# Block-causal attention and gated MLP on one core: maxima over partitions taken by GpSimd instead of TensorE matmuls, scales of q, k and v formed from the maximum itself

## The chip, the cores and the metric

The kernel runs on one core of a Trainium2 chip. The metric is device time in microseconds (us) of one execution, the median of the runs. One core has five engines that matter here, each with its own instruction queue that runs strictly in order: TensorE (PE in the profile; its weight loads stand apart as PEld), VectorE (DVE), ScalarE (ACT), GpSimd (POOL) and SyncE (SP), which only issues DMA transfers. TensorE writes its results to PSUM; VectorE and ScalarE take them from there.

## The reference

```
scores = scale * q @ k.T                      # per batch (8) and head (8), 576 x 576, head size 64
scores = where(block_i >= block_j, scores, -1e9)   # blocks of 64
attn   = softmax(scores);  a = attn @ v
x      = a as (8*576 tokens, 512)
h      = x @ w_in                             # 512 -> 2048
out    = (h * clip(h + 3, 0, 6) / 6) @ w_out  # 2048 -> 512
```

q, k, v and the output are float32. The weights arrive as 64-bit floats, and the kernel itself converts them.

## The kernel before, in words

**Precision.** Most of the work runs as float16 products in three terms: an operand x is scaled, split into a high part hi = f16(x*s) and a low part lo = f16(x*s - hi), and a product becomes hi*hi + hi*lo + lo*hi. The scale s of each operand is made on the chip, from the data: for each pair of heads for q and k, for each batch for v, for each of 8 chunks of the two weight matrices. The first batch (and the first piece of the MLP) runs in float32 without scales, while the weights are still being converted.

**Stages.** There are 8 batches of 4 head pairs: 32 slots, n = 0 to 31. Slots 0 to 3 take the float32 path (`qk_load32`, `qk_prep32`, `s_block32`, `t_block32`, `pv_group32`). Slots 4 to 31 take the float16 path: `qk_load` loads q and k of a head pair; `qk_prep` makes the scales, splits q and k and sends them through a transposing DMA to the tile qkT; `s_group` forms the scores on TensorE (tile s), takes row maxima on VectorE (st), the exponentials on ScalarE (p), splits the probabilities (ph, phl) and transposes them by DMA (pT); `v_max` and `v_prep` scale and split v (vhl); `pv_group` multiplies (pv) into x. The tokens are cut into 13 pieces for the MLP: `ffn1` forms h (tile h; from piece 10 on by seven products in place of eight, tile u, from sums made by `w_forms` and `x_forms` on VectorE), `ffn2` the output (o, osb). The attention of later batches and the MLP of earlier ones run side by side, so that TensorE always has one of them.

**The order.** No engine chooses its order on the chip. The function emits its operations to a `Recorder`, each with a due time (`nc.key`, from the tables and constants at the top of the file: `AT` for the slots, `FT` for the pieces, `QP`, `VP`, `M0`, `S0` and so on as offsets), and with a cost that the planner holds for it. `Recorder.schedule` (lines 296 to 492) simulates the engines with these costs and writes one fixed order for each; an operation that can run on several engines goes to the one that the plan finds free first. All engine instructions but the first memsets are issued from line 498, so the profile names them L498 and is read by tile names.

**The scales.** `pow2_scale` (line 569) makes a scale from the per-partition figures mx of 128 partitions and one or two columns. Everything that follows needs the same value in each partition. In `qk_prep` mx is the sum of absolute values of each partition, made by ScalarE; for v and the weights it is the true maximum (v) or again a sum (weights):

- q and k (`exact=False`): one joint pair of small float32 matmuls with a matrix of ones adds mx over the partitions into PSUM (tile mb_q); then VectorE, in its queue: `am` (lower bound), `pw` (exponent bits alone, a power of two), `rs` twice (product with 2^-14, reciprocal), and `esc` (the factor of the exponent).
- v and weights (`exact=True`): a pair of matmuls with the identity first transposes mx (mt_v, mt_w), VectorE takes the maximum along the row (`dg`) and spreads it on a diagonal, a second pair with ones brings it to all partitions (mb_v, mb_w), and the same chain follows.

With the 16 scales of v and w and the 28 of q and k, 44 scales are made. The option `far`, by DMA through memory, is never taken (`WFAR, VFAR = 99, 99`). GpSimd has only memsets to do: the zero halves of the float32 q tiles (`qkf`, at the start), and zero blocks of the probabilities (`pf`, `p`).

`w_max` calls `pow2_scale` for a chunk of weights, `w_split` uses the result; their due times are M0 + i*MD and S0 + i*SD for i = 0 to 7. `qk_prep` of slot n is due QP slots ahead of its `s_group`, `v_prep` VP slots behind the slot's start.

Of the kernel before, what the change touches and what calls it, by code (L numbers as in the profile page):

```python
# [10 lines left out]
F32 = mybir.dt.float32  # L11
# [3 lines left out]
ALU = mybir.AluOpType  # L15
AX = mybir.AxisListType

P = 128
# [4 lines left out]
WX = 14  # L23
WY = 27

U = 0.632
AS = (6.363, 13.291, 20.163, 24.432)
AL = 17.497
PV0 = 2.428
TA, TR, PR = 2.701, 4.807, 2.397  # L30
QR = 4.605
PVA, PVB = 0.974, 1.579
PHS = 18
WLP = 0
WHA = 0
EXA = 8
QTH = False
EVR = 3
EVP = 0
PRO = True  # L40
MEM = 0
BIASV = 262.216
WFAR, VFAR = 99, 99
SW = 10
WF0, WFD = 768.607, 15.583
XFA = 10.306

NMIN = 64
QL = -4.051
VL = -0.654  # L50
W0, WD = 11.216, 2.584
S0, SD = 56.335, 3.846
M0, MD = 33.747, 5.394
RT = (28.905, 39.268, 48.982, 59.104)
RS, RL, VL1 = 1.915, 15.575, 37.318
VM0, VMX = 80.864, 0.114
AT = ((4, 86.25), (5, 104.31), (6, 123.19), (8, 163.76), (9, 178.32), (10, 199.81), (12, 251.29), (13, 269.94), (14, 285.88), (15, 306.89), (16, 332.9), (24, 564.98), (32, 785.9))
FT = ((0, 34), (1, 120.0), (2, 165.17), (3, 233.37), (4, 273.76), (5, 348.85), (6, 400.52), (7, 495), (10, 765), (13, 965.63))
UNI = False
QP = 0.642  # L60
VP = 0.443
BLK = 64
EXPONENT_BITS = 0x7F800000

# [19 lines left out]
        return call  # L84


ADV = {("tensor", "a"): 51.29}


class Recorder:  # L90
# [15 lines left out]
    def __init__(self, nc):  # L106
        self.nc = nc
        self.ops = []
        self.key = 0.0
        self.cls = ""  # L110
        self.joint = None
        self.adv = ADV
        self.BIAS = {"vector": BIASV, "gpsimd": 500.0}
        for n in self.NAMES:
            setattr(self, n, Engine(self, n))
        self.hist = {}
        self.meta = {}
        self.users = {}
# [121 lines left out]
    def cost(self, eng, method, args, kw, outs, ins):  # L240


        n = self.count(outs[0])
        if method == "dma_start":
            nb = mybir.dt.size(outs[0].dtype)
            for _, c in list(outs[0].ap):
                nb *= c
            if kw.get("transpose"):
                occ = max(1290, 189 * nb / 32768 - 200)
                return occ, occ + (1100 if nb <= 4 * 32768 else 2100), False  # L250
            if eng == "gpsimd":
                return 1300, 2900 + nb / 170, False
            return 600, 2000 + nb / 170, False
        if eng == "vector":
            if method == "tensor_reduce":
                n = self.count(ins[0])
            else:
                ptr = any(isinstance(a, bass.AP) and self.count(a) == 1 for a in args[2:] if n > 1)
                ptr = ptr or n == 1 and method == "tensor_scalar_mul" and isinstance(args[2], bass.AP)
            wide = [a for a in ins if self.count(a) > 1 and not self.psum(a)]  # L260
            port = len(wide) > 1
            if method in ("tensor_scalar", "tensor_copy") and n > 1:
                if not any(self.psum(a) for a in outs + ins):
                    if len(outs[0].ap) == 2 or outs[0].ap[1][1] % 2 == 0:
                        n = n / (4 if mybir.dt.size(outs[0].dtype) + mybir.dt.size(ins[0].dtype) == 4 else 2)
                        port = True
            occ = 68 + 1.042 * n
            if method != "tensor_reduce" and ptr:
                occ += 57
            return occ, occ + 80, port  # L270
        if eng == "scalar":
            occ = 94 + 0.8335 * n
            if isinstance(kw.get("scale"), bass.AP):
                occ += 95
            if isinstance(kw.get("bias"), bass.AP):
# [226 lines left out]
def kernel(  # L502
# [13 lines left out]
    nc = Recorder(tc.nc)  # L516
    B, H, S, D = q.shape
# [23 lines left out]
    E_P = 2.0 ** 14  # L541
    E_X = 2.0 ** -14
    E_G = 2.0 ** -25
    C_EXP = (D ** -0.5) * 2.0 ** -28
    C_H = 2.0 ** -28
    C_O = 2.0 ** -17 / 6.0
    TINY = 1e-18


# [2 lines left out]
    natp = ctx.enter_context(tc.tile_pool(name="nat", bufs=2))  # L552
    attp = ctx.enter_context(tc.tile_pool(name="att", bufs=2))
    ffp = ctx.enter_context(tc.tile_pool(name="ff", bufs=3))
    drp = ctx.enter_context(tc.tile_pool(name="dr", bufs=2, space=bass.MemoryType.DRAM))
    ps_s = ctx.enter_context(tc.tile_pool(name="ps_s", bufs=3, space=bass.MemoryType.PSUM))
    ps_h = ctx.enter_context(tc.tile_pool(name="ps_h", bufs=2, space=bass.MemoryType.PSUM))
    ps_o = ctx.enter_context(tc.tile_pool(name="ps_o", bufs=1, space=bass.MemoryType.PSUM))
# [7 lines left out]
    ph01 = [wpool.tile([P, 2, PT_U[g], P], F16, tag=f"ph{g}", name=f"ph{g}") for g in range(2)]  # L566
    padded = []

    def pow2_scale(mx, n, nm, to=None, exact=False, far=False):

# [7 lines left out]
        if exact and far:  # L578
            row = drp.tile([n, P], F32, tag=f"row{n}", name=f"dr_row_{nm}")
            nc.sync.dma_start(row.rearrange("n p -> p n"), mx)  # L580
            al = sm.tile([P, n, P], F32, tag="al", bufs=1, name=f"al_{nm}")
            nc.sync.dma_start(
                al.rearrange("p n x -> p (n x)"),
                row.rearrange("n p -> (n p)").rearrange("(o x) -> o x", o=1).to_broadcast([P, n * P]),
            )
            nc.vector.tensor_reduce(am, al, axis=AX.X, op=ALU.max)
            nc.vector.tensor_scalar_max(am, am, TINY)
        else:
            if exact:
                pt_ = ps_s.tile([P, 512], F32, tag="s", name=f"mt_{nm}")  # L590
                nc.joint = "mt", nm
                for h in range(2):
                    wide = mx[:, h % n:h % n + 1].to_broadcast([P, BLK])
                    nc.tensor.matmul(pt_[h * BLK:(h + 1) * BLK, :P], wide, ident, start=True, stop=True)
                nc.joint = None
                dg = sm.tile([P, n + 1], F32, tag=f"dg{n}", name=f"dg_{nm}")
                nc.vector.tensor_reduce(dg[:, n:], pt_[:, :P], axis=AX.X, op=ALU.max)
                nc.vector.tensor_scalar_mul(dg[:, :n], ident[:, :(n - 1) * BLK + 1:BLK], dg[:, n:])
                mx = dg[:, :n]
            ps = ps_s.tile([P, 512], F32, tag="s", name=f"mb_{nm}")  # L600
            nc.joint = "mb", nm
            for h in range(2):
                nc.tensor.matmul(ps[h * BLK:(h + 1) * BLK, :n], ones[:, :BLK], mx, start=True, stop=True)
            nc.joint = None
            nc.vector.tensor_scalar_max(am, ps[:, :n], TINY)
        nc.vector.tensor_scalar(
            pw.bitcast(I32), am.bitcast(I32), EXPONENT_BITS, None, op0=ALU.bitwise_and
        )
# [26 lines left out]
    ones = one.to_broadcast([P, P])  # L635
    three = wpool.tile([P, 1], F32, tag="three", name="three")
    nc.gpsimd.memset(three, 3.0)
    n_raw = []
# [71 lines left out]
    def w_max(c):  # L710

        acc = sm.tile([P, 2], F32, tag="wm", name=f"wm{c}")
        for wi, w in enumerate("io"):
# [4 lines left out]
        pow2_scale(acc, 2, f"w{c}", (pwio[:, c], rsio[:, c]), exact=True, far=c >= WFAR)  # L718

    def w_split(c):  # L720

# [52 lines left out]
    def v_max(n):  # L774
# [8 lines left out]
        if hp == NPAIR - 1:  # L783
            m1 = sm.tile([P, 1], F32, tag="vm1", name=f"vm1_{b}")
            nc.vector.tensor_reduce(m1, vmax[b], axis=AX.X, op=ALU.max)
            vscale[b] = pow2_scale(m1, 1, f"v{b}", exact=True, far=b >= VFAR)

    def v_prep(n):
        t = vnat[n % NVB]
# [36 lines left out]
    def qk_prep(n):  # L826
# [3 lines left out]
        for s in range(2):  # L830
# [6 lines left out]
        nc.vector.scalar_tensor_tensor(  # L837
            sc[:, 0:1], pw[:, 0:1], C_EXP, pw[:, 1:2], op0=ALU.mult, op1=ALU.mult
        )
        esc[n] = sc  # L840

        nc.scaled(sp[:, 0, :, 0], t[:, 0], rs[:, 0:1], "AV")
# [39 lines left out]
    def qk_prep32(n, rest):  # L882
# [3 lines left out]
        if not rest:  # L886
# [16 lines left out]
            for qd in parts[1:]:  # L903
# [2 lines left out]
                nc.gpsimd.memset(qd[BLK:, :, 0], 0.0)  # L906
                for i in range(qd.shape[1]):
                    qkT[n][1].append((qd, i))
        kT, qd = qkT[n]
        c0, c1 = (T0, S) if rest else (0, T0)  # L910
        if rest:
# [29 lines left out]
    def s_block32(n, i):  # L941
# [25 lines left out]
        pr = attp.tile([P, NJ * P], F32, tag="p", bufs=NPB, name=f"pf{n}_{i}")  # L967

        if nk % P:
            nc.gpsimd.memset(pr[:, nk:nk + BLK], 0.0)  # L970
        sm_ = sums[n, g][:, ii:ii + 1]
        for ci, (c0, c1) in enumerate(chunks):
            nc.scalar.activation(
# [271 lines left out]
    acc = {}  # L1245
# [452 lines left out]
```

## Time and profile before

| | us |
|---|---|
| median of 3 runs | 967.64 (966.87 to 967.70) |
| the profiled execution, its own time | 968.66 |
| its span, first to last instruction | 966.9 |
| PE busy | 954.4 (99%) |
| DVE busy | 838.0 (87%) |
| ACT busy | 704.6 (73%) |
| POOL busy | 18.3 (2%) |

Busy time of PE is a union of modelled spans: matmuls are pipelined, and the span of one reaches into the next. What a group costs TensorE is therefore read from the starts: from its own first start to the first start of the group behind it. The granted TensorE clock was 1.00 in the whole span.

### The profile page before, as it was taken

To read this page: it belongs to the slowest core of one execution; us is meant where nothing else is said; L and a number is where in the kernel's file an instruction comes from. 1 tells how busy PE (TensorE), PEld (TensorE's weight loads), DVE (VectorE), ACT (ScalarE), POOL (GpSimd) and SP (SyncE) were. 2 spreads that over 40 slices of the span, in tenths; PEclk is the share of its full clock that TensorE was granted. 3 is DMA by queue.
4 is the path that set the end of the run, shared out by engine and by line. 5 is a ranking of instruction groups with operands and counts; after the bars stand their busy time and mean duration, and the time that the engine had idled before them with its cause. 6 is when DMAs were issued, how large, how long until landed. Compare 5 with 4: busy or idle time off the path is not lost. (4 is left out here: it accounts for less than half of the span.)

```text
span 966.9 us, 30947 instructions
## 1 busy us (share of the span) xinstructions
PE 954.4 (99%) x12604; PEld 709.2 (73%) x12604; DVE 838.0 (87%) x2240; ACT 704.6 (73%) x1838; POOL 18.3 (2%) x101
## 2 busy tenths in 40 slices
PE   8999999999999999999999999999999999999998
PEld 6655456877778877777666667777887677888886
DVE  6899999999899999989799889788889997765654
ACT  6889768888887887878677777787888754454433
POOL 3000000000000000000000000000000000000000
PEclk9999999999999999999999999999999999999999
DMA  7975879999879989998797889787866300000000
GB/s 183 251 235 175 199 133 167 170 184 184 158 135 197 182 168 147 174 172 153 118 190 146 146 177 148 141 164 141 134 141 109 72 13 24 3 35 2 35 3 34
DMA packets 414351, 129.03 MB, mean 133 GB/s; under 512 B 403200, under 2 KB 403712, under 8 KB 414208
## 3 DMA queue, kind: packets, MB, share of 16 engines
q1 hardware_dynamic: 414064, 126.92, 68.0%
q8 instruction: 99, 1.62, 0.7%
q14 instruction: 44, 0.36, 0.1%
q10 hardware_dynamic: 144, 0.13, 0.0%
HBM read 45.09 MB, written 9.44 MB: 56 GB/s over the span
## 5 line engine op out<-in xcount | busy, mean ns | idle before, releaser
L498 PE MATMUL o<-wout,g 128*64 128x512 f16 (+3 forms) x3418 | 420.6, 383 | 0.2 <-DVE osb L498 0.2
L498 PE MATMUL h<-x,win 128*64 128x384 f16 (+3 forms) x3640 | 332.0, 318 | 0.1
L498 PEld LDWEIGHTS <-g 128*64 128x64 f16 x3264 | 211.7, 110 | 103.8 <-issue 0.4
L498 PEld LDWEIGHTS <-win 128*64 128x64 f16 x4320 | 246.0, 110 | 47.6 <-issue 0.2
L498 ACT ACTIVATE p<-s,st,esc 128x64 f32<-128x64 f32 (+1 forms) x280 | 162.8, 586 | 8.7 <-DVE ph L498 4.2
L498 DVE TENSOR_REDUCE st<-s 128x1 f32<-128x64 f32 (+1 forms) x280 | 116.2, 445 | 3.6 <-PE s L498 3.4
L498 ACT ACTIVATE r<-h,eg,sh 128x192 f32<-128x192 f32 (+1 forms) x176 | 98.1, 577 | 20.3 <-PE h L498 19.3
L498 DVE SCALAR_TENSOR_TENSOR g<-r,g 128x384 f16<-128x384 f32 (+1 forms) x192 | 98.7, 517 | 7.7 <-ACT g L498 6.0
L498 ACT ACTIVATE g<-r 128x384 f16<-128x384 f32 (+1 forms) x146 | 71.9, 494 | 38.1 <-DVE r L498 33.0
L498 DVE SCALAR_TENSOR_TENSOR r<-r,eg,h 128x384 f32<-128x384 f32 (+1 forms) x144 | 80.5, 561 | 19.5 <-ACT r L498 19.4
L498 PE MATMUL s<-qkT 128*64 128x64 f16 (+7 forms) x1120 | 94.8, 287 | 0.1
L498 PEld LDWEIGHTS <-vhl 128*64 128x64 f16 x1680 | 73.2, 110 | 12.8 <-issue 4.6
L498 PE MATMUL pv<-pT,vhl 128*64 128x192 f16 (+2 forms) x1680 | 73.8, 233 | 0.8 <-DMA pT<-ph 0.7
L498 PEld LDWEIGHTS <-qkT 128*64 128x64 f16 x1120 | 58.5, 111 | 20.8 <-issue 3.6
L498 ACT ACTIVATE st<-st,esc 128x1 f32<-128x1 f32 (+2 forms) x129 | 36.9, 291 | 41.8 <-DVE st L498 41.3
L498 DVE SCALAR_TENSOR_TENSOR ph<-p,st,ph 128x256 f16<-128x256 f32 (+2 forms) x168 | 66.7, 443 | 0.0
L498 DVE SCALAR_TENSOR_TENSOR phl<-p,st,phl 128x512 f16<-128x512 f32 (+1 forms) x84 | 62.5, 789 | 0.0
L498 ACT ACTIVATION_READ_ACCUMULATOR p<-s,st,esc 128x1 f32 x280 | 55.1, 197 | 0.0
L498 ACT ACTIVATE ph<-p,st 128x64 f16<-128x64 f32 (+5 forms) x109 | 44.1, 449 | 9.7 <-DVE st L498 9.2
L498 PEld LDWEIGHTS <-wf 128*64 128x64 f16 x1152 | 48.8, 110 | 0.7 <-DVE ph L498 0.5
L498 DVE SCALAR_TENSOR_TENSOR qks<-qk,rs_q,qks 128x576 f16<-128x576 f32 x56 | 43.8, 808 | 0.0
L498 DVE TENSOR_TENSOR ph<-u,ph 128x384 f32<-128x384 f32 (+1 forms) x48 | 24.3, 506 | 20.4 <-PE u L498 18.7
(179 smaller groups left out, 1135.4 us busy)
## 6 DMA issues: line engine op xcount, KB each, us to landing
out_dram<-osb SPq DMA_DIRECT2D x34, 256.0 KB, 2.6
vnat<-in_v_dram SPq DMA_DIRECT2D x64, 128.0 KB, 2.9
qk<-in_q_dram SPq DMA_DIRECT2D x28, 288.0 KB, 3.7
qk<-in_k_dram SPq DMA_DIRECT2D x28, 288.0 KB, 4.3
rawi<-in_moe_w_in_dram SPq DMA_DIRECT2D x8, 512.0 KB, 4.3
rawo<-in_moe_w_out_dram SPq DMA_DIRECT2D x8, 512.0 KB, 4.7
ph<-in_moe_w_in_dram SPq DMA_DIRECT2D x6, 512.0 KB, 4.5
ph<-in_moe_w_out_dram SPq DMA_DIRECT2D x6, 512.0 KB, 4.6
```

Source lines behind the costliest of these rows:

```text
L498: getattr(eng, method)(*args, **kw)
```

## The change

`pow2_scale` no longer uses TensorE. GpSimd's `partition_all_reduce` takes the maximum over the 128 partitions and leaves it in each of them. For q, k and v a scale is no longer a power of two: `pw` is the maximum times 2^-15, and `rs` its reciprocal; `pw` and the exponent's factor `esc` are made by GpSimd, only the reciprocal by VectorE. The weights keep their power of two, by the same VectorE chain, from the maximum that GpSimd leaves in SBUF. For q and k the figure is now the largest of the per-partition sums, not their total. One all-reduce on a column of ones (`al_one`) is put behind the memsets of slot 0's q tile. The planner's cost of an all-reduce is 3,000 ns, and 12,000 ns for the first. The zero blocks `pf` of the first batch may now be set by GpSimd or VectorE. The constants that follow from the scales change with them (C_H, C_O, E_V), and the due times and planner's constants at the top of the file are others. The unused path through memory is removed with its pool.

```
-U = 0.632                          +U = 0.694
-AL = 17.497                        +AL = 22.827
-QR = 4.605                         +QR = 4.343
-PV0 = 2.428                        +PV0 = 1.766
-PVA, PVB = 0.974, 1.579            +PVA, PVB = 0.839, 1.931
-BIASV = 262.216                    +BIASV = 257.139
-WF0, WFD = 768.607, 15.583         +WF0, WFD = 773.481, 13.439
-XFA = 10.306                       +XFA = -10.514
-W0, WD = 11.216, 2.584             +W0, WD = 11.453, 2.397
-S0, SD = 56.335, 3.846             +S0, SD = 58.514, 0.3
-M0, MD = 33.747, 5.394             +M0, MD = 32.922, 4.385
-RS, RL, VL1 = 1.915, 15.575, 37.318   +RS, RL, VL1 = 1.724, 13.104, 30.526
-VM0, VMX = 80.864, 0.114           +VM0, VMX = 79.88, 0.059
-QP = 0.642                         +QP = 0.551
-VP = 0.443                         +VP = 0.355
 (AT: slots 9 to 32 about 3 us later; FT: single points by up to 5.5 us; RT, TA, TR, PR by tenths)
...
+            if method == "partition_all_reduce":
+                took = 3000.0 if self.awake else 12000.0
+                self.awake = True
+                return took, took + 30, False
...
-    C_EXP = (D ** -0.5) * 2.0 ** -28
-    C_H = 2.0 ** -28
-    C_O = 2.0 ** -17 / 6.0
+    E_V = 2.0 ** 15
+    C_H = 2.0 ** -14
+    C_O = 2.0 ** -3 / 6.0
...
-            if exact:
-                pt_ = ps_s.tile([P, 512], F32, tag="s", name=f"mt_{nm}")
-                nc.joint = "mt", nm
-                for h in range(2):
-                    wide = mx[:, h % n:h % n + 1].to_broadcast([P, BLK])
-                    nc.tensor.matmul(pt_[h * BLK:(h + 1) * BLK, :P], wide, ident, start=True, stop=True)
-                nc.joint = None
-                dg = sm.tile([P, n + 1], F32, tag=f"dg{n}", name=f"dg_{nm}")
-                nc.vector.tensor_reduce(dg[:, n:], pt_[:, :P], axis=AX.X, op=ALU.max)
-                nc.vector.tensor_scalar_mul(dg[:, :n], ident[:, :(n - 1) * BLK + 1:BLK], dg[:, n:])
-                mx = dg[:, :n]
-            ps = ps_s.tile([P, 512], F32, tag="s", name=f"mb_{nm}")
-            nc.joint = "mb", nm
-            for h in range(2):
-                nc.tensor.matmul(ps[h * BLK:(h + 1) * BLK, :n], ones[:, :BLK], mx, start=True, stop=True)
-            nc.joint = None
-            nc.vector.tensor_scalar_max(am, ps[:, :n], TINY)
+        al = sm.tile([P, n], F32, tag=f"al{n}", name=f"al_{nm}")
+        nc.gpsimd.partition_all_reduce(al, mx, P, bass_isa.ReduceOp.max)
+        if nm[0] != "w":
+            nc.gpsimd.tensor_scalar(pw, al, TINY, 1.0 / E_V, op0=ALU.max, op1=ALU.mult)
+            nc.vector.reciprocal(rs, pw)
+            return pw, rs
+        nc.vector.tensor_scalar_max(am, al, TINY)
...
-        nc.vector.scalar_tensor_tensor(
-            sc[:, 0:1], pw[:, 0:1], C_EXP, pw[:, 1:2], op0=ALU.mult, op1=ALU.mult
-        )
+        nc.gpsimd.tensor_tensor(sc[:, 1:2], pw[:, 0:1], pw[:, 1:2], op=ALU.mult)
+        nc.gpsimd.tensor_scalar(sc[:, 0:1], sc[:, 1:2], D ** -0.5, 1.0, op0=ALU.mult, op1=ALU.mult)
...
+            if not n:
+                nc.key += 0.01
+                al = sm.tile([P, 1], F32, tag="al1", name="al_one")
+                nc.gpsimd.partition_all_reduce(al, one, P, bass_isa.ReduceOp.max)
...
-            nc.gpsimd.memset(pr[:, nk:nk + BLK], 0.0)
+            nc.add([(e, "memset", (pr[:, nk:nk + BLK], 0.0), {}) for e in ("gpsimd", "vector")])
```

More of the change, by code (lines that the diff above doesn't have):

```diff
@@ L24 @@
 WY = 27
-U = 0.632
+U = 0.694
 AS = (6.363, 13.291, 20.163, 24.432)
[L28 to L32, printed above, removed]
+AL = 22.827
+PV0 = 1.766
+TA, TR, PR = 2.61, 5.437, 2.53
+QR = 4.343
+PVA, PVB = 0.839, 1.931
 PHS = 18
@@ L38 @@
 EVR = 3
-EVP = 0
+EVP = 2
 PRO = True
 MEM = 0
-BIASV = 262.216
-WFAR, VFAR = 99, 99
+BIASV = 257.139
 SW = 10
-WF0, WFD = 768.607, 15.583
-XFA = 10.306
+WF0, WFD = 773.481, 13.439
+XFA = -10.514
 NMIN = 64
[L49 to L58, printed above, removed]
+QL = -4.064
+VL = -0.221
+W0, WD = 11.453, 2.397
+S0, SD = 58.514, 0.3
+M0, MD = 32.922, 4.385
+RT = (28.905, 38.922, 48.125, 59.128)
+RS, RL, VL1 = 1.724, 13.104, 30.526
+VM0, VMX = 79.88, 0.059
+AT = ((4, 86.25), (5, 104.31), (6, 123.19), (8, 163.76), (9, 181.37), (10, 202.86), (12, 254.34), (13, 272.99), (14, 288.93), (15, 310.36), (16, 335.95), (24, 568.03), (32, 788.95))
+FT = ((0, 34), (1, 120.0), (2, 165.17), (3, 238.88), (4, 273.76), (5, 348.85), (6, 401.03), (7, 494.75), (10, 764.04), (13, 965.73))
 UNI = False
-QP = 0.642
-VP = 0.443
+QP = 0.551
+VP = 0.355
 BLK = 64
@@ L84, in __getattr__ @@
         return call
-ADV = {("tensor", "a"): 51.29}
+ADV = {("tensor", "a"): 56.01}
 class Recorder:
@@ L115, in __init__ @@
             setattr(self, n, Engine(self, n))
+        self.awake = False
         self.hist = {}
@@ L554 @@
     ffp = ctx.enter_context(tc.tile_pool(name="ff", bufs=3))
-    drp = ctx.enter_context(tc.tile_pool(name="dr", bufs=2, space=bass.MemoryType.DRAM))
     ps_s = ctx.enter_context(tc.tile_pool(name="ps_s", bufs=3, space=bass.MemoryType.PSUM))
@@ L567, with pow2_scale @@
     padded = []
-    def pow2_scale(mx, n, nm, to=None, exact=False, far=False):
+    def pow2_scale(mx, n, nm, to=None):
         if to:
@@ L577, in pow2_scale @@
         am = sm.tile([P, n], F32, tag=f"am{n}", name=f"am_{nm}")
[L578 to L584, printed above, removed]
-            )
-            nc.vector.tensor_reduce(am, al, axis=AX.X, op=ALU.max)
-            nc.vector.tensor_scalar_max(am, am, TINY)
-        else:
-            if exact:
-                pt_ = ps_s.tile([P, 512], F32, tag="s", name=f"mt_{nm}")
-                nc.joint = "mt", nm
-                for h in range(2):
-                    wide = mx[:, h % n:h % n + 1].to_broadcast([P, BLK])
-                    nc.tensor.matmul(pt_[h * BLK:(h + 1) * BLK, :P], wide, ident, start=True, stop=True)
-                nc.joint = None
-                dg = sm.tile([P, n + 1], F32, tag=f"dg{n}", name=f"dg_{nm}")
-                nc.vector.tensor_reduce(dg[:, n:], pt_[:, :P], axis=AX.X, op=ALU.max)
-                nc.vector.tensor_scalar_mul(dg[:, :n], ident[:, :(n - 1) * BLK + 1:BLK], dg[:, n:])
-                mx = dg[:, :n]
-            ps = ps_s.tile([P, 512], F32, tag="s", name=f"mb_{nm}")
-            nc.joint = "mb", nm
-            for h in range(2):
-                nc.tensor.matmul(ps[h * BLK:(h + 1) * BLK, :n], ones[:, :BLK], mx, start=True, stop=True)
-            nc.joint = None
-            nc.vector.tensor_scalar_max(am, ps[:, :n], TINY)
+        al = sm.tile([P, n], F32, tag=f"al{n}", name=f"al_{nm}")
[5 more added lines that the diff above has]
+        nc.vector.tensor_scalar_max(am, al, TINY)
         nc.vector.tensor_scalar(
@@ L634 @@
     nc.gpsimd.memset(one, 1.0)
-    ones = one.to_broadcast([P, P])
     three = wpool.tile([P, 1], F32, tag="three", name="three")
@@ L717, in w_max @@
             nc.scalar.activation(ab, c32, AF.Abs, accum_out=acc[:, wi:wi + 1])
-        pow2_scale(acc, 2, f"w{c}", (pwio[:, c], rsio[:, c]), exact=True, far=c >= WFAR)
+        pow2_scale(acc, 2, f"w{c}", (pwio[:, c], rsio[:, c]))
     def w_split(c):
@@ L785, in v_max @@
             nc.vector.tensor_reduce(m1, vmax[b], axis=AX.X, op=ALU.max)
-            vscale[b] = pow2_scale(m1, 1, f"v{b}", exact=True, far=b >= VFAR)
+            vscale[b] = pow2_scale(m1, 1, f"v{b}")
     def v_prep(n):
@@ L836, in qk_prep @@
         sc = sm.tile([P, 2], F32, tag="esc", bufs=3, name=f"esc{n}")
-        nc.vector.scalar_tensor_tensor(
-            sc[:, 0:1], pw[:, 0:1], C_EXP, pw[:, 1:2], op0=ALU.mult, op1=ALU.mult
-        )
+        nc.gpsimd.tensor_tensor(sc[:, 1:2], pw[:, 0:1], pw[:, 1:2], op=ALU.mult)
+        nc.gpsimd.tensor_scalar(sc[:, 0:1], sc[:, 1:2], D ** -0.5, 1.0, op0=ALU.mult, op1=ALU.mult)
         esc[n] = sc
```

## The prediction

> **What bounds the kernel now.** I read first the page's busy shares, then the busy time of the engines in four stretches (after the stretch its length, then us of PE, PEld, DVE, ACT and POOL).
>
> ```profile
> span 966.9 us, 30947 instructions
> PE 954.4 (99%) x12604; PEld 709.2 (73%) x12604; DVE 838.0 (87%) x2240; ACT 704.6 (73%) x1838; POOL 18.3 (2%) x101
> ...
> 0.00:20.00 20.00, 15.23 (x85) 11.21 (x86) 12.41 (x38) 12.31 (x39) 7.47 (x32) 1.00 0.69 164
> 20.00:80.00 60.00, 58.95 (x401) 37.48 (x402) 54.91 (x159) 52.93 (x137) 2.25 (x13) 1.00 0.81 242
> 80.00:800.00 720.00, 717.62 (x9553) 530.06 (x9551) 667.01 (x1845) 567.62 (x1527) 8.62 (x56) 1.00 0.82 150
> 800.00:967.00 167.00, 162.64 (x2576) 130.47 (x2572) 103.67 (x201) 71.77 (x137) 0.00 (x0) 1.00 0.06 19
> ```
>
> TensorE is covered without a gap but for 4.8 us in the first 20 us and 4.4 us after 800. A busy PE need not be at its peak, so I looked at the starts of its groups in the timeline, in the middle of the kernel, where one of the removed matmul groups (mb_q) stands.
>
> ```profile
> 503.26 2.11 PE L498 MATMUL o<-wout,g 128*64 128x512 f16 x18
> 505.20 0.23 PE L498 MATMUL mb_q<-qkmx,one 128*64 128x2 f32 x4
> 505.29 0.39 PE L498 MATMUL s<-qkT 128*64 128x256 f16 x4
> 505.51 1.15 PE L498 MATMUL h<-x,win 128*64 128x384 f16 x12
> ...
> 529.30 0.23 PE L498 MATMUL mb_q<-qkmx,one 128*64 128x2 f32 x4
> ...
> 955.36 6.49 PE o L498 x60
> ```
>
> Eighteen o matmuls take 505.20 - 503.26 = 1.94 us, 0.108 us each. The chain's last row has the same where nothing competes: 6.49 / 60 = 0.108. So TensorE runs at its own pace in the middle, and each instruction taken from its queue shortens the end by its step, unless a new wait appears. **VectorE is the next bound:** busy 667 of the 720 us from 80 to 800, 53 us free.
>
> **What is removed from TensorE.** A group's step is the difference between its start and the next group's. For mb_q that is 505.29 - 505.20 = 0.09 us, though its busy time reads 0.23. The weights' groups stand here:
>
> ```profile
> 54.00 0.39 PE L498 MATMUL mt_w<-ident,wm 128*64 128x128 f32 x4
> 54.22 0.82 PE L498 MATMUL h<-x,win 128*64 128x384 f32 x4
> ...
> 55.94 0.23 PE L498 MATMUL mb_w<-dg_w,one 128*64 128x2 f32 x4
> 56.03 0.84 PE L498 MATMUL h<-x,win 128*64 128x384 f32 x4
> ```
>
> mt_w costs 0.22, mb_w 0.09. The counts come from the groups by shape, four records to a group:
>
> ```profile
> L498 PE MATMUL mb_q<-qkmx,one 128*64 128x2 f32 x112 | 7.1, 185 | 1.3 <-ACT qks L498 1.3
> L498 PE MATMUL mt_w<-ident,wm 128*64 128x128 f32 x32 | 3.3, 282 | 0.0
> L498 PE MATMUL mt_v<-ident,vm 128*64 128x128 f32 x32 | 3.2, 275 | 0.0
> L498 PE MATMUL mb_v<-dg_v,one 128*64 128x1 f32 x32 | 2.1, 189 | 0.0
> L498 PE MATMUL mb_w<-dg_w,one 128*64 128x2 f32 x32 | 2.0, 185 | 0.3 <-DVE dg_w L498 0.3
> ```
>
> That is 28 mb_q, 8 each of the others: 28 x 0.09 + 16 x 0.22 + 16 x 0.09 = 2.5 + 3.5 + 1.4 = **7.5 us**. Adding their busy times would give 17.7, but most of each lies under its neighbours; that is the upper end of this term, the steps are what I take. The idle time before them goes too, 1.3 + 0.3 = **1.6 us**: in-order TensorE waited there for a sum from ScalarE and a maximum from VectorE. PSUM slots that these groups held for the scores come free as well; I put no number on that.
>
> **What is removed from VectorE**, and what stays:
>
> ```profile
> L498 DVE TENSOR_SCALAR pw_q<-am_q 128x2 int32<-128x2 int32 x28 | 4.4, 159 | 0.1
> L498 DVE TENSOR_SCALAR rs_q<-pw_q 128x2 f32<-128x2 f32 x28 | 4.4, 158 | 0.1
> L498 DVE RECIPROCAL rs_q<-rs_q 128x2 f32<-128x2 f32 x28 | 4.3, 152 | 0.0
> L498 DVE SCALAR_TENSOR_TENSOR esc<-pw_q 128x1 f32<-128x1 f32 x28 | 4.2, 150 | 0.0
> L498 DVE TENSOR_SCALAR am_q<-mb_q 128x2 f32<-128x2 f32 x28 | 4.1, 148 | 0.0
> L498 DVE TENSOR_REDUCE dg_v<-mt_v 128x1 f32<-128x128 f32 x8 | 2.3, 283 | 0.1
> L498 DVE TENSOR_REDUCE dg_w<-mt_w 128x1 f32<-128x128 f32 x8 | 2.2, 280 | 0.0
> ```
>
> For a slot am, pw, the product rs and esc go, 0.62 us; the reciprocal stays. In all 17.1 us for q and k and 4.5 us for the two reductions (the small rest of v and w left out). VectorE is not the bound now, so this is worth nothing by itself; it is cover for what follows.
>
> **What is added on GpSimd.** 44 all-reduces and a first one, and for q, k and v small element-wise steps. No all-reduce stands in this trace. These are the nearest rows: GpSimd's start, and from the transfers the one kind that also carries data across partitions.
>
> ```profile
> 1.00 0.29 POOL masks.py:199 TENSOR_SCALAR_AFFINE_SELECT ident<-ident 128x128 f32<-128x128 f32 x1
> ...
> 1.96 1.20 POOL L498 MEMSET qkf<- 64x576 f32 x2
> 3.21 0.33 POOL L498 MEMSET pf<- 128x64 f32 x3
> 3.46 3.93 POOL L498 MEMSET qkf<- 64x576 f32 x8
> ...
> qkT<-qks SPq DMA_TRANSPOSE x28, 7.6
> ```
>
> So one costs between 0.29 us (a single pass of GpSimd) and 7.6 us (through the DMA engines and back); I take the planner's 3.0, between them, because the order is written for it: what matters is a departure from it. With 3.0 and three small steps of about 0.3, GpSimd has some 4 us per slot of 24.1 us (529.30 - 505.20), and nothing but memsets beside it: hidden. The wait that the change adds is the reciprocal's. VectorE's queue stands still there until GpSimd is done, and behind it are row maxima of scores, splits of probabilities and the MLP's g, for which ScalarE, the transposes and TensorE wait in turn. By the plan it is placed behind the end of the reduction; I take zero. The transfers stay the same in number; the 28 qkT transposes stay behind the splits in SP's queue, so a late scale also delays the loads behind them.
>
> **The first all-reduce** has a place of its own. It goes behind slot 0's memsets, which end at 1.96 + 1.20 = 3.16 us, and ahead of those of slots 1 to 3. Slot 1's scores need slot 1's memsets:
>
> ```profile
> 14.78 0.94 PE L498 MATMUL sf<-qkf 128*128 128x128 f32 x6
> ```
>
> If the first call lasts 12 us as planned, those memsets (1.2 us) end at 3.2 + 12 + 1.2 = 16.4, and slot 1's scores start 1.6 us late, with hardly any other work on TensorE there. Bounds: 0 (a short call) and 9.2 (a call one transpose's time, 7.6 us, beyond the plan). I take **+1.6**. The Trainium skill (GPSIMD Engine Reference, section Instruction dispatch) gives about 6 us for a first call of freshly loaded code; with 6 the memsets would end at 10.4 and this term would be zero. No run here shows which.
>
> **What is moved.** The pf memsets may go to VectorE: at most 3 us in the first 80 us, where VectorE has 12.7 us free; cost zero. The weights' maxima come earlier (the last is due at 63.6 for 71.5), and so do their splits (60.6 for 83.3); q and k's preparation 2.2 us later (0.091 of a slot), v's 2.1 us earlier. These reorder VectorE's work and add none: between -2 and +2, taken as zero. `x_forms` of the last pieces is due 20.8 us later, where VectorE is tight:
>
> ```profile
> 700.00:800.00 100.00, 99.98 (x1386) 73.50 (x1384) 97.19 (x226) 71.78 (x178) 0.60 (x4) 1.00 0.43 82
> L498 DVE TENSOR_TENSOR xt<-xs,xt 128x384 f16<-128x384 f32 x12 | 6.4, 543 | 0.0
> ```
>
> A piece has four such and four like them, 8 x 0.54 = 4.3 us, that TensorE would stand still for if they came too late: 0 to 4.3 once, taken as zero, since 0.62 us a slot has come free there.
>
> **The sum**, on the profiled execution's own 968.66 (1.76 outside its span): 968.66 - 7.5 - 1.6 + 1.6 = 961.2. The median of the runs is 1.0 lower, 967.64, and gives 960.1. I predict **960.6**.
>
> **Rivals.** *The gain fills up again.* The lead of q and k's preparation falls to 0.551 x 24.1 = 13.3 us, and 7.6 of it is the transpose. If each slot's scores or its reciprocal wait 0.25 us more, 28 x 0.25 = 7 us: about 967.5, no change. For it: mb_q already had a wait of 1.3. Against it: TensorE has MLP work to go on with.
>
> *VectorE stands at the reciprocal (slower).* Per slot it has 53 / 30 = 1.8 us free and 0.62 freed, 2.4 in all. If a reduction lasts 3.0 us longer than the plan, 28 x (3.0 - 2.4) = 17 us come on top: 978. It decides from 28 x (x - 2.4) = 7.5, x = 2.7, that is a reduction of 5.7 us.
>
> *The first call is long (slower).* Each us beyond 12 is a us for TensorE; at 25 us the term is 14.6: 974. It decides from 12 + 7.5 = 19.5 us.
>
> *GpSimd locks VectorE out.* About 35 reductions fall between 80 and 800 us, 35 x 3.0 = 105 us. If VectorE stood still in all of it, 105 - 53 - 22 = 30 us come on top: 991; if in two thirds or less, it is hidden. The trace has only memsets there, so it is silent. The Trainium skill (SBUF — State Buffer, section Who interferes with whom) says that a VectorE instruction with two SBUF inputs or in a two-port mode and a GpSimd instruction that reads SBUF exclude each other for the whole instruction; no run here shows it yet.
>
> **How the numbers follow.** Forecast 0.68, with its own range 956 to 965 (reordering and x_forms up, a short first call and freed slots down); gain filled up 0.12; VectorE at the reciprocal 0.08; long first call 0.07; lock 0.05. What can be told from no change is 0.2%, 965.7 to 969.6. Faster 0.69 (the forecast, and the mild ends of others), same 0.12, slower 0.19. The range reaches from 955 over the filled-up case into the mild slower ones, 970.
>
> **What would show it.** Right: no mb or mt groups on PE, steps of o still 0.108, VectorE busy about 815, PE's busy total lower, the middle still without gaps. Wrong: idle time before RECIPROCAL rs_q that ends on POOL; sf of slot 1 far behind 16.4 us; longer g, qks or phl on VectorE beside a reduction; PE idle before u ended by VectorE. The prediction fails if all-reduces last over 5.7 us or the first over 19.5.

## The result, and the profile after

| | before | after |
|---|---|---|
| median | 967.45 us (966.87 to 967.70, 4 runs) | 1155.83 us (1151.55 to 1160.27, 4 runs) |
| profiled execution, its own time | 968.66 | 1160.27 |
| span | 966.9 | 1158.5 |

The changed kernel is slower by a factor of 1.194 (95% interval 1.192 to 1.196). The prediction was 960.6 in a range of 955 to 970. The page of the changed kernel begins:

```profile
span 1158.5 us, 30428 instructions
...
PE 1008.9 (87%) x12304; PEld 745.9 (64%) x12304; DVE 829.2 (72%) x2085; ACT 710.8 (61%) x1833; POOL 66.9 (6%) x230
...
PEclk9898899898899998999899889889899999999999
```

Two things are new. TensorE is idle for 1158.5 - 1008.9 = 149.6 us, where it was idle for 12.5 before: 137.1 us more. And it is busy for 54.5 us more, though instructions were taken from it: the row of the clock, all nines before, has eights in it. 137.1 + 54.5 = 191.6, the whole difference of the spans. The stretches (length, then PE, PEld, DVE, ACT, POOL busy, the granted clock) show where:

```profile
0.00:20.00 20.00, 14.21 (x82) 10.47 (x83) 11.08 (x37) 11.07 (x34) 6.78 (x25) 1.00 0.66 146
...
80.00:800.00 720.00, 601.65 (x7084) 434.13 (x7084) 503.77 (x1325) 450.31 (x1198) 47.70 (x159) 0.91 0.67 127
800.00:1000.00 200.00, 184.95 (x2450) 142.84 (x2448) 168.98 (x404) 133.57 (x343) 7.82 (x28) 0.97 0.50 95
```

It is the whole range of the float16 slots, at a clock of 0.91. The start is nearly as before. GpSimd's timeline shows what it does, here in one stretch (start and length in us, engine, line, operation, what it writes and reads, how many; in brackets the engine's idle time before it and what ended it):

```profile
109.66 0.37 POOL L502 PARTITION_ALL_REDUCE al_v<-vm  x1 [1.32 <-DVE vm L502]
117.05 0.27 POOL L502 TENSOR_SCALAR pw_v<-al_v 128x1 f32<-128x1 f32 x1 [7.02 <-issue]
123.45 0.37 POOL L502 PARTITION_ALL_REDUCE al_q<-qkmx  x1 [6.13 <-ACT st L502]
131.31 0.26 POOL L502 TENSOR_SCALAR pw_q<-al_q 128x2 f32<-128x2 f32 x1 [7.48 <-issue]
131.65 0.19 POOL L502 TENSOR_TENSOR esc<-pw_q 128x1 f32<-128x1 f32 x1
```

Every instruction is short, 0.4 us for an all-reduce. But between an all-reduce and the element-wise instruction behind it stand 7 us that end on "issue", that is on nothing that the profile shows, and before the next all-reduce another 6, which here may be a wait for its data as well; the first all-reduce of all, on ready data, ran 5.75 us late. Who waits is told by the waits (engine and tile, who it waited for, us in total, times, longest):

```profile
POOL pw_q L502 <- issue: 202.9, 28, 7.9
DVE rs_q L502 <- POOL pw_q L502: 157.0, 27, 9.8
ACT qks L502 <- DVE rs_q L502: 101.6, 17, 9.3
PE s L502 <- ACT p L502: 47.6, 20, 6.9
```

GpSimd spends 202.9 / 28 = 7.2 us a slot in this gap. VectorE stands in it at the reciprocal, 157 us in 27 waits, and ScalarE behind VectorE. The last row is TensorE's largest: the exponentials (p) that it waits for stand in ScalarE's queue behind qks; near 460 us ScalarE waits 7.32 us at qks, and TensorE 6.91 us for a p behind it. Another such place, on VectorE and then on TensorE:

```profile
189.33 0.41 DVE L502 SCALAR_TENSOR_TENSOR r<-r,eg,h 128x192 f32<-128x192 f32 x1
199.59 0.17 DVE L502 RECIPROCAL rs_q<-pw_q 128x2 f32<-128x2 f32 x1 [9.85 <-POOL pw_q L502]
199.79 0.52 DVE L502 TENSOR_SCALAR qks<-qk,rs_q 128x576 f16<-128x576 f32 x1
```

```profile
196.13 0.84 PE L502 MATMUL o<-wout,g 128*64 128x512 f16 x6
206.30 0.64 PE L502 MATMUL s<-qkT 128*64 128x256 f16 x4 [9.33 <-DVE x L502]
```

VectorE stands still for 9.85 us; TensorE runs out of work 7 us later and is idle for 9.33; from 204 to 208 us its granted clock is 0.50. In the row of the waits it is a VectorE tile (x) that ends TensorE's wait: x stood in VectorE's queue behind the reciprocal.

**Is the reduction slow, or what follows it?** The weights' reductions are taken by VectorE, not by GpSimd. First GpSimd's timeline, then VectorE's:

```profile
46.52 0.37 POOL L502 PARTITION_ALL_REDUCE al_w<-wm  x1 [7.98 <-ACT pT L502]
46.77 0.31 POOL L502 MEMSET pf<- 128x64 f32 x2
```

```profile
46.93 0.17 DVE L502 TENSOR_SCALAR am_w<-al_w 128x2 f32<-128x2 f32 x1 [2.19 <-POOL al_w L502]
```

VectorE, which was waiting, reads the result 0.41 us after the reduction began, and GpSimd itself goes on with a memset at once. So this reduction is done in 0.4 us. In GpSimd's instruction queue a kind stands that was there twice in the kernel before:

```profile
L502 POOLq MODIFY_POOL_CONFIG  x140: 4/11/85, 3.4 to 902.4; - x140
```

That is 140, or 70 pairs. GpSimd's timeline has, memsets aside, just 70 places where an all-reduce and an element-wise instruction follow each other, 35 in each direction: one pair for each. My theory from here on: **GpSimd loads other code at each such change, which takes some 5.8 us towards the all-reduce and 7.2 us back; the reduction costs 0.4 us.** Rival 1: the result of a reduction comes 7 us late for whoever takes it (the row above speaks against it). Rival 2: the new due times are at fault. And whether it is the place in VectorE's order or the longer way that costs is open.

### The profile page after: what moved, and what is told of

It reads as the page before. It is cut to its first block, busy times and chain, and to the rows that moved or that the text cites. A ratio compares the mean times of both kernels' runs of the same rounds, so it can differ in the third digit from the quotient of the medians.

```text
span 1158.5 us, 30428 instructions
## 1 busy us (share of the span) xinstructions
PE 1008.9 (87%) x12304; PEld 745.9 (64%) x12304; DVE 829.2 (72%) x2085; ACT 710.8 (61%) x1833; POOL 66.9 (6%) x230
## 5 line engine op out<-in xcount | busy, mean ns | idle before, releaser
L502 PE MATMUL o<-wout,g 128*64 128x512 f16 (+3 forms) x3402 | 435.6, 390 | 11.4 <-DVE g L502 7.1
L502 PE MATMUL h<-x,win 128*64 128x384 f16 (+3 forms) x3618 | 354.4, 334 | 13.1 <-DVE r L502 9.1
L502 PEld LDWEIGHTS <-win 128*64 128x64 f16 x4320 | 268.4, 115 | 62.7 <-issue 13.0
L502 PEld LDWEIGHTS <-g 128*64 128x64 f16 x3264 | 224.4, 113 | 117.0 <-issue 14.2
L502 PE MATMUL s<-qkT 128*64 128x64 f16 (+7 forms) x1120 | 107.2, 306 | 81.7 <-ACT p L502 47.6
L502 PEld LDWEIGHTS <-qkT 128*64 128x64 f16 x1120 | 63.0, 116 | 114.5 <-issue 80.4
L502 DVE RECIPROCAL rs_q<-pw_q 128x2 f32<-128x2 f32 x28 | 4.6, 166 | 157.0 <-POOL pw_q L502 157.0
L502 ACT ACTIVATE qks<-qk,rs_q 128x576 f16<-128x576 f32 x21 | 16.1, 773 | 101.6 <-DVE rs_q L502 101.6
L502 DVE SCALAR_TENSOR_TENSOR ph<-p,st,ph 128x256 f16<-128x256 f32 (+3 forms) x168 | 67.6, 447 | 0.1
L502 ACT ACTIVATE ph<-p,st 128x256 f16<-128x256 f32 (+5 forms) x102 | 42.8, 462 | 12.0 <-DVE st L502 11.6
```

The source lines that it names most:

```text
L502: getattr(eng, method)(*args, **kw)
```

## The experiments

In all of them the computation is the reference's, unless the text says otherwise. Each result stands with the kernel before timed on the same chip.

**1. The scales by VectorE.** Only all-reduces and memsets stay on GpSimd.

```
-            nc.gpsimd.tensor_scalar(pw, al, TINY, 1.0 / E_V, op0=ALU.max, op1=ALU.mult)
+            nc.vector.tensor_scalar(pw, al, TINY, 1.0 / E_V, op0=ALU.max, op1=ALU.mult)
...
-        nc.gpsimd.tensor_tensor(sc[:, 1:2], pw[:, 0:1], pw[:, 1:2], op=ALU.mult)
-        nc.gpsimd.tensor_scalar(sc[:, 0:1], sc[:, 1:2], D ** -0.5, 1.0, op0=ALU.mult, op1=ALU.mult)
+        nc.vector.scalar_tensor_tensor(
+            sc[:, 0:1], pw[:, 0:1], D ** -0.5, pw[:, 1:2], op0=ALU.mult, op1=ALU.mult
+        )
```

> The changed kernel, but the lower bound, the product with 2^-15 (pw) and the exponent's factor (esc) are made by VectorE, so that GpSimd has all-reduces and memsets alone. Theory (GpSimd changes its code between an all-reduce and an element-wise instruction, 5.8 us in and 7.2 us out, the reduction itself takes 0.4 us): no gap behind the all-reduces, VectorE waits under 1 us per slot, the granted clock is 1.00 again, 956 to 966 us. Rival 1 (the result of a reduction is late, whoever takes it): VectorE waits some 6 us at each pw, 1100 to 1160 us. Rival 2 (the new due times and order are at fault): over 1100 us as well, but without that wait.

Measured: 982.36 us (981.00 to 983.06), ratio 1.0152 (1.0137 to 1.0167). Of the 188 us 173 are gone. VectorE's idle time before rs_q is 0.2 us in all. Rival 1 is out, and rival 2 as the main cause, since the due times are those of the changed kernel. The expected 956 to 966 was missed all the same. GpSimd's start and TensorE's waits tell why:

```profile
8.50 0.28 POOL masks.py:199 TENSOR_SCALAR_AFFINE_SELECT ident<-ident 128x128 f32<-128x128 f32 x1 [7.57 <-issue]
```

```profile
PE o L502 <- ACT g L502: 9.8, 1, 9.8
PE qt L502 <- POOL ident masks.py:199: 8.8, 1, 8.8
```

The affine select that builds the identity waited 7.57 us on "issue" at the very start; in the changed kernel it began at 1.23. TensorE's first transposes come at 8.8 in place of 4.0. And TensorE stood still once for 9.8 us from 800.1 us on, with a granted clock of 0.50 in the 5.9 us behind it. VectorE is busy for 9.8 of the 10.0 us from 798.2 to 808.2, almost only with sums of weights (w, ws, wf of `w_forms`); the r and g that TensorE waits for stand behind them in its order. In between TensorE has small idle times:

```profile
200.00:400.00 200.00, 195.29 (x2798) 147.38 (x2795) 182.01 (x506) 165.41 (x459) 7.90 (x29) 0.99 0.95 167
```

4.8 + 9.8 + 4.7 = 19.3 us; by this sum it would be 963 without them.

**2. The whole change with the old due times**, that is the constants of the kernel before from U to VP and the lead ADV.

> The whole change in the functions, but the due times and constants at the top of the file (U to VP, and the lead of TensorE's attention work) as before the change. Theory of changed code: GpSimd's pairs of changes stay, 1120 to 1200 us. Rival 2 (due times): back near the kernel before, 960 to 975 us.

Measured: 1126.34 us, ratio 1.1629 (1.1597 to 1.1661). The new tables are not the cause; 30 us of the 188 hang on how they meet the stalls.

**3. A plan that knows.** The planner's cost of an all-reduce is 400 ns, and its schedule adds the change of code whenever the kind of instruction on GpSimd changes:

```
+            if e == "gpsimd" and calls[0][0] != "memset":
+                lib = calls[0][0] == "partition_all_reduce"
+                if lib != self.awake:
+                    self.awake = lib
+                    occ, took = occ + (5800.0, 7100.0)[not lib], took + (5800.0, 7100.0)[not lib]
```

> The changed kernel, with the planner told what the trace shows: 0.4 us for an all-reduce, 5.8 us more when it follows an element-wise instruction on GpSimd, 7.1 us more when an element-wise instruction follows it. If the loss is only the place of the reciprocal in VectorE's order (work behind it stands still): VectorE's wait at rs_q falls from 157 us to under 40 and the time to 965 to 1000 us. If the longer way to the scale itself (13 us for a slot of 24) is what costs, whatever stands where: 1050 us or more.

Measured: 1088.62 us, ratio 1.1260 (1.1234 to 1.1286). The wait moved as expected:

```profile
DVE rs_q L505 <- POOL pw_q L505: 34.8, 13, 7.6
```

from 157 us to 34.8, but the time came down by 67 us only and stays above the 1050 us that were expected if the longer way to the scale is what costs. So an order that knows the changes takes back about a third of the loss. The rest, with these due times, I put down to the longer way to each scale; that is by exclusion and not shown by itself.

**4. The single costs.** The output is filled with zeros and nothing of the reference is computed; GpSimd runs chains of small instructions, and TensorE bursts of 56 matmuls of 512 columns, each burst behind a longer chain on VectorE.

```
+    for i in range(3):
+        x = ar(x, "arB")
...
+    for i in range(3):
+        x = ts(x, "tsC")
...
+    for i in range(3):
+        x = act(ar(x, "arD"), "acD")
+        x = act(ts(x, "tsD"), "acE")
+    for i in range(2):
+        x = act(ar(x, "arF"), "acF")
+        nc.gpsimd.memset(m, 0.0)
```

> None of the computation: the output is filled with zeros, and chains of small instructions are run on GpSimd, then bursts of 56 matmuls on TensorE with growing idle times between them. Theory of changed code: three all-reduces one behind the other, each on the result of the last, come under 1 us apart; three element-wise instructions likewise; in the alternating chain every step costs 5.5 to 7.5 us; a memset between two all-reduces costs nothing like that; a reduction of 128 columns costs a few us at most. Rival 1: dependent all-reduces are 7 us apart. For TensorE: if idle time takes the clock away, bursts after idle times over some 3 us start at half speed, and those after shorter ones don't.

GpSimd's timeline (ar: all-reduces, ts: element-wise, ms: memsets):

```profile
2.73 0.36 POOL L89 PARTITION_ALL_REDUCE arB<-acA  x1 [0.33 <-ACT acA L99]
3.18 0.80 POOL L89 PARTITION_ALL_REDUCE arB<-arB  x2
10.86 0.26 POOL L94 TENSOR_SCALAR tsC<-acB 128x2 f32<-128x2 f32 x1 [6.88 <-issue]
11.21 0.52 POOL L94 TENSOR_SCALAR tsC<-tsC 128x2 f32<-128x2 f32 x2
18.55 0.37 POOL L89 PARTITION_ALL_REDUCE arD<-acC  x1 [6.82 <-issue]
25.86 0.26 POOL L94 TENSOR_SCALAR tsD<-acD 128x2 f32<-128x2 f32 x1 [6.95 <-issue]
32.18 0.37 POOL L89 PARTITION_ALL_REDUCE arD<-acE  x1 [6.06 <-issue]
...
59.43 0.22 POOL L116 MEMSET msF<- 128x64 f32 x1
59.90 0.35 POOL L89 PARTITION_ALL_REDUCE arF<-acF  x1 [0.24 <-ACT acF L99]
```

Three dependent all-reduces are 0.4 us apart, three element-wise instructions 0.3; over the whole chain a change takes 6.0 to 6.8 us towards the all-reduce and 6.7 to 7.0 us back; a memset between two all-reduces changes nothing. So the cost in the theory is measured by itself. What GpSimd does in that time no trace shows: the pages' rows of instruction transfers did not grow with the 70 changes (q8: 96 packets, 99 before; q14: 45, 44 before). "Loads code" is a name for it here. The Trainium skill (GPSIMD Engine Reference, section Instruction dispatch) knows an instruction-memory load of about 6 us at the first call of a freshly loaded kernel, without a visible instruction; the trace agrees with the size, and shows that here it is paid at every change, in both directions. TensorE's timeline of the same run:

```profile
46.56 12.26 PE L127 MATMUL ps<-mv,wt 128*128 128x512 f16 x56 [2.02 <-DVE wt L134]
61.47 13.95 PE L127 MATMUL ps<-mv,wt 128*128 128x512 f16 x56 [2.65 <-DVE wt L134]
...
113.38 13.95 PE L127 MATMUL ps<-mv,wt 128*128 128x512 f16 x56 [3.82 <-DVE wt L134]
132.07 14.96 PE L127 MATMUL ps<-mv,wt 128*128 128x512 f16 x56 [4.74 <-DVE wt L134]
```

After 1.05 to 2.02 us of idle time a burst takes 12.26 us; after 2.65 to 3.82 us it takes 1.7 us more, after 4.74 us 2.7 more. The granted clock is 1.00 in the first 3.4 us of the burst at 46.56, 0.65 in those of the burst at 61.47 and 0.50 at 132.07. So a stall of TensorE can be paid twice: once as idle time, once at a lower clock behind it. The Trainium skill (TensorE: Matmul & The Clock Gate, section What's actually happening) has the clock halved after an idle window of about 3.4 us that runs freely. By an estimate from that page's figure a window at half clock loses 1.7 us, so the size agrees; but here 2.65 us of idle time were enough. The length of a wait alone does not decide it: in run 2 the granted clock stayed at 1.00 behind a wait of 3.31 us (to 805.96), in run 12 it was 0.52 in the 3.3 us behind one of 2.14 us (to 34.06). In the changed kernel 24 of TensorE's waits last 2.65 us or more, 104 us in all.

**5. What an execution leaves behind.** As 1, with one element-wise instruction of GpSimd at the very end, that nobody waits for.

```
     nc.emit()
+    last = sm.tile([P, 1], F32, tag="last", name="last")
+    tc.nc.gpsimd.tensor_scalar(last, one, 1.0, 1.0, op0=ALU.mult, op1=ALU.mult)
```

> As e1_vec, and one element-wise instruction on GpSimd behind everything else, that nobody waits for. In e1_vec GpSimd's affine select at the start waited 7.6 us for nothing that the profile shows, in the changed kernel it did not. Theory: the code that an execution leaves loaded is still there in the next; e1_vec ends with the all-reduce's, the changed kernel with the element-wise one's. Then the first transposes on TensorE come at 4.0 us again in place of 8.8, and the time is 4 to 8 us under e1_vec's 982. Rival: the 7.6 us belong to the program as loaded: no change, 980 to 984.

Measured: 977.85 us (977.39 to 978.65), 4.5 under run 1, no overlap. The start is back:

```profile
1.21 0.29 POOL masks.py:199 TENSOR_SCALAR_AFFINE_SELECT ident<-ident 128x128 f32<-128x128 f32 x1 [0.29 <-POOL ident masks.py:197]
```

An instruction at the end of one execution moved the start of the next: what GpSimd has loaded outlives the execution. The changed kernel did not suffer from it because its last GpSimd arithmetic was element-wise.

**6. The due times alone.** The kernel before, with all its matmuls, and the constants of the changed kernel.

> The kernel before, with its matmuls for the maxima, but with the due times and constants of the changed kernel. If the tables are harmless by themselves: 965 to 972 us. If the 9.8 us for which TensorE stood at the last pieces in e1_vec comes from the tables (x_forms due 20.8 us later): 975 to 990 us, with an idle time of TensorE near 800 us.

Measured: 971.61 us, ratio 1.0042 (1.0027 to 1.0057). No idle time near 800 us: the 9.8 us of run 1 do not come from the tables by themselves.

**7 and 8. The old due times with the scales on VectorE**, and a planner's cost of 500 ns for an all-reduce and 6,000 for the first; 8 has the instruction at the end as well.

> As e1_vec (all-reduces on GpSimd, everything else of the scales on VectorE), but with the due times of the kernel before, and a planner's cost of 0.5 us for an all-reduce (6 for the first). The prediction's sum without the tables and without the changes of code: 968.7 - 7.5 - 1.6, and 5 us more for the late identity at the start as in e1_vec: 962 to 968 us. If the tables cost nothing in e1_vec, it is 980 again.

> As e7_old_vec, with the element-wise instruction on GpSimd at the end as in e5_vec_end. If both the code left loaded and the removed matmuls are as held: 957 to 962 us, under the kernel before by 6 to 10. If the code at the start is not what was late: as e7_old_vec.

Measured: 970.89 us for 7, 3 us above the stretch that was expected, ratio 1.0027 (1.0015 to 1.0039); 966.03 us for 8, ratio 0.9980 (0.9970 to 0.9990). The instruction at the end is worth 4.9 us again. Number 8 is the fastest here, by 0.1 to 0.3%: hardly more than can be told from no change, and 4 us above the stretch that was expected. Its stretch from 80 to 260 us, and a place in it:

```profile
80.00:260.00 180.00, 175.93 (x2086) 122.14 (x2086) 170.59 (x466) 146.69 (x384) 11.72 (x30) 0.99 0.94 174
```

```profile
199.98 0.85 PE L503 MATMUL pv<-pT,vhl 128*64 128x192 f16 x18
203.69 0.74 PE L503 MATMUL s<-qkT 128*64 128x320 f16 x4 [2.86 <-DVE x L503]
```

TensorE waits 2.86 us for VectorE there, and the granted clock is 0.54 in the 3.4 us behind it. Over the span TensorE is 5.6 us less busy than before (948.8 for 954.4), but 3.4 us more idle: 2.2 us remain, the difference of the spans.

**9. The number of changes, off the way to the reciprocal.** As 7, with esc on GpSimd again and pw on VectorE.

> As e7_old_vec, but the factor of the exponent (esc, a product of two columns and one with a constant) is made by GpSimd again, as in the change; the lower bound and pw stay on VectorE. GpSimd changes its code twice a slot as in the changed kernel, but nobody waits for the way back except esc, which is due at the slot's scores. If the number of changes is what costs: 1050 us or more. If it is only the change on the way to the reciprocal: near e8_old_vec_end, 964 to 975 us, with no wait of VectorE for GpSimd over 2 us a slot. (The last instruction of GpSimd is element-wise by itself, so no start-up wait.)

Measured: 1007.92 us, ratio 1.0417 (1.0393 to 1.0442); neither 1050 nor 975. The stretches:

```profile
80.00:150.00 70.00, 53.84 (x310) 27.12 (x310) 46.08 (x110) 38.35 (x84) 5.07 (x15) 0.85 0.57 139
150.00:820.00 670.00, 660.29 (x8938) 504.19 (x8936) 596.87 (x1583) 518.34 (x1411) 42.69 (x135) 0.99 0.82 146
820.00:1006.00 186.00, 170.29 (x2660) 123.59 (x2655) 120.30 (x233) 79.75 (x150) 0.00 (x0) 0.96 0.05 19
```

From 150 to 820 us TensorE is idle for 9.7 us, with two changes of code in each slot going on: there the number of changes costs little. 16.2 us of idle time stand between 80 and 150, where weights' reductions come right behind esc and wait for the change towards the all-reduce:

```profile
90.76 0.37 POOL L503 PARTITION_ALL_REDUCE al_w<-wm  x1 [5.89 <-issue]
97.94 0.19 POOL L503 TENSOR_SCALAR esc<-esc 128x1 f32<-128x1 f32 x1 [6.81 <-issue]
104.03 0.37 POOL L503 PARTITION_ALL_REDUCE al_w<-wm  x1 [5.90 <-issue]
```

```profile
DVE am_w L503 <- POOL al_w L503: 19.7, 3, 7.2
```

VectorE, which takes the weights' maxima itself, stands three times at am_w, at 91.2, 104.4 and 133.0 us, and TensorE's three long waits of the stretch, 4.8, 6.0 and 5.3 us, end at 94.1, 106.2 and 139.6, behind them. So a change on the way to a result that VectorE needs costs here too. One more wait, of 11.3 us, stands before 834, like the one in run 1: VectorE is busy for 9.2 of the 9.4 us from 823.0 to 832.4, again with the sums of weights of `w_forms` ahead of the r and g that TensorE waits for. Why these crowd there in some orders and not in others I have not found.

**10. Without the first all-reduce on ones.** As 8, without `al_one`.

> e8_old_vec_end without the first all-reduce on a column of ones. If it hides anything, the first reduction for v pays the change of code of some 6 us at 23 us of the span: VectorE's scale for v comes 6 us later, 966 to 972 us. If GpSimd does the change ahead, while it waits for the maximum anyway: the same as e8_old_vec_end within 2 us.

Measured: 971.64 us, ratio 1.0042 (1.0025 to 1.0058). That is in the stretch expected if the first all-reduce hides the change. But the first reduction for v comes at 24.28 us, not later than in 8 (24.68):

```profile
24.28 0.74 POOL L503 PARTITION_ALL_REDUCE al_v<-vm  x1 [5.57 <-DVE qkf L503]
```

```profile
L503 POOLq MODIFY_POOL_CONFIG  x6: 6/11/83, 18.7 to 136.5; - x6
```

GpSimd's queue reached the change at 18.7 us, and the reduction began 5.57 us behind the last memset. Its maximum (vm) was ready at 22.93. So GpSimd made 4.2 us of the change while it waited for the maximum, and 1.35 us were left to pay; in 8, where the first all-reduce had made the change, al_v starts 0.1 us behind its maximum. The 5.6 us are not lost there but in single stalls of TensorE near 146, 208 and 227 us, in another order of work. The longest, 3.37 us at 146.44, is a change of code once more: the plan gave one scaling of q and k (qks, at 135.22) to GpSimd, which began it 7.50 us behind an all-reduce; SyncE waits 5.2 us for it with the transpose, ScalarE 5.25 us for the transpose, and TensorE for the exponentials behind that. So the first all-reduce by itself hides little.

**11. Other due times for number 8**: first loads, weights' maxima, v's preparation and a few points of AT and FT.

```
-U = 0.632        +U = 0.658
-AL = 17.497      +AL = 21.855
-W0, WD = 11.216, 2.584     +W0, WD = 11.262, 2.584
-M0, MD = 33.747, 5.394     +M0, MD = 33.747, 6.293
-VP = 0.443       +VP = 0.371
...
```

> e8_old_vec_end with some twenty of the due times set anew for this set of costs (first loads, weights' maxima, v's preparation 0.371 of a slot ahead, the spacing of the first batch). In e8 2.9 us of idle time and 3.4 us at half clock near 203 us eat most of the removed 7.5 us. If that stall is a matter of the order alone: 957 to 962 us. If a stall of this size comes with the reductions themselves: 964 to 968 us again.

Measured: 966.84 us, in the second of the stretches expected, ratio 0.9985 (0.9975 to 0.9994). The stall of 2.86 us at 203 us is gone; smaller ones, of 0.95 to 1.32 us, came in its place at 193, 204, 298 and 312 us.

**12. Less work on VectorE.** As 8, with the figures of v made by ScalarE (`VM_ACT = 32` in place of 0); sums of absolute values, still an upper bound for the scale.

> e8_old_vec_end with the figures of v taken by ScalarE (sums of absolute values, as for q and k) in place of VectorE's reductions, 32 of 0.81 us: 26 us less on VectorE, spread over the slots, about as much more on ScalarE, which has more room. If VectorE, busy 96% of the time from 80 to 260 us, is what holds the removed 7.5 us of TensorE back: 958 to 963 us. If it is the order of single waits and not VectorE's load: 964 to 970 us, as e8_old_vec_end.

Measured: 969.23 us, ratio 1.0016 (1.0007 to 1.0025). This settles less than I wanted. The stretch, to set beside that of number 8:

```profile
80.00:260.00 180.00, 177.73 (x2148) 122.61 (x2145) 171.20 (x475) 151.41 (x405) 9.15 (x29) 1.00 0.93 178
```

VectorE is busy for 171.2 us of the 180, where it was 170.6 in number 8: the planner gave it other instructions in exchange (over the span its busy time fell by 8 us, not 26). In that stretch TensorE is idle for 2.3 us in place of 4.1; but it lost more than that before 80 us (71.96 us busy, 74.43 in number 8), where it waits 2.14 us at 34 us and loses the clock behind it. So the run shows no gain from this edit, but it does not show what a lighter VectorE would do in that stretch.

## Why the prediction was wrong

**The step that failed** is "What is added on GpSimd": one price for an all-reduce, 3.0 us between 0.29 and 7.6, and "some 4 us per slot ... hidden". The reduction was cheaper than that, 0.4 us. What the step did not have is a price for the neighbourhood: an all-reduce and an element-wise instruction side by side cost 5.8 us one way and 7.2 the other, 13 us a slot. So the wait that the same step put at zero, the reciprocal's ("I take zero"), came to 157 us on VectorE. I had priced the new instructions one by one, from rows of single instructions, and the step lists both kinds in one sentence. The trace of before could not show the change: in it GpSimd runs memsets and one affine select.

**The rival "VectorE stands at the reciprocal" is what happened**, with its place, its queue and its sign, idle time before the reciprocal that ends on GpSimd. It had 0.08. That it named the place was not knowledge of the cause: its condition was a reduction of over 5.7 us, and the reduction took 0.4; the 7.2 us stood behind it. Its size was off for two reasons. Measured are 157 us over 27 waits, 5.8 us each; by the rival's formula, with 2.4 us of cover a slot, 28 x (5.8 - 2.4) = 95 us. TensorE's idle time grew by 137.1. VectorE's free 1.8 us a slot were an average over many short gaps (206 from 80 to 800 us in the kernel before, the longest 2.41 us); a single wait does not find them in one place. And the stalls took the clock: TensorE's busy time grew by 54.5 us although 7.5 us of steps left it, and the granted clock of the profiled execution was 0.937. The prediction read the clock of 1.00 as given; it gave no rival a price for the clock.

**The removed matmuls** were sized rightly, as far as number 8 shows. It has the whole removal and no change of code on the way, and TensorE is busy 5.6 us less, though some 1.6 us (3.4 us at a clock of 0.54) are lost behind the stall at 203 us: 7.2 against 7.5. But a shorter queue of TensorE did not shorten the end as much: 3.4 us came back as idle time, 2.2 remain of 9.1 (7.5 and the 1.6 of waits). "Each instruction taken from its queue shortens the end by its step, unless a new wait appears": they appeared, in 8, 11 and 12 at other places each time. Whether they come from VectorE, at 95% in that stretch, or from the order, runs 11 and 12 did not settle; it stays open.

**The first all-reduce** was put at 12 us and +1.6 us for the end. It ran at 9.15 us, 5.75 behind the memsets; in number 8, which has it too, TensorE is busy in the first 20 us as long as in the kernel before (15.23 us), and slot 1's scores, at 15.40 us, wait for nothing. The term was zero. It would have been zero, too, with the 6 us of the Trainium skill (GPSIMD Engine Reference, section Instruction dispatch), as the prediction says.

**GpSimd locks VectorE out**: no. In the changed kernel 43 of VectorE's instructions with two tensor inputs ran beside a reduction, and none was over 10 ns longer than the median of its kind. But it can be the reduction that waits:

```profile
139.21 1.28 DVE L502 SCALAR_TENSOR_TENSOR win<-win,rsio 128x1024 f16<-128x1024 f32 x1
```

```profile
139.60 1.12 POOL L502 PARTITION_ALL_REDUCE al_w<-wm  x1 [7.47 <-ACT abo L502]
```

It ends 0.24 us behind VectorE's instruction. 15 of the 45 reductions last over 0.5 us, up to 1.12, and beside each of them VectorE ran such an instruction or a scaling of one tensor; the median of all is 0.38 us. That is small beside the 7.2 us.

**The due times** were taken as zero between -2 and +2, and x_forms as 0 to 4.3; alone, on the kernel before, they cost some 4 us (run 6).

## What to carry to other kernels

Before GpSimd gets work of a new kind, list all that it runs in order, and count how often the kind changes between library routines such as the all-reduce and its element-wise arithmetic: on this chip each change cost 6 to 7 us, memsets excepted, while the reduction itself cost 0.4. Keep one kind on GpSimd and give the small arithmetic around it to the engine that takes the result. And price a stall of TensorE from some 2 us on with the clock that it may lose, not as idle time alone (2.02 us kept the clock in run 4; 2.14 us lost it in run 12).

## What the runs showed of the hardware that I had not expected

- What GpSimd has loaded outlives an execution: the last GpSimd instruction of one execution decided whether the first affine select of the next waited 7.57 us or nothing (runs 1 and 5; again 7 and 8, 4.9 us).
- The change towards an all-reduce begins when GpSimd's queue reaches it, while the all-reduce still waits for its data (run 10: 4.2 of 5.57 us lay under that wait). The change back stands between the reduction and the scale that needs it, and is paid in full (7.2 us in the mean over the 28 slots of the changed kernel).
- An all-reduce over 128 partitions of two columns takes 0.4 us from its start to the instruction of another engine that reads it (46.52 to 46.93 us), and up to 1.12 us beside some VectorE instructions.
